# Decayed keys on ScalarE, a reordered first block, a new order of loads and state products behind the attention of step 1

## Chip, cores, metric

The kernel runs on one core of one Trainium2 chip. The metric is the device time of one execution in microseconds (us), the median of several executions. The profiled execution has a span (first to last instruction) that is some 2 us shorter than the time of the same execution. All runs that are compared here are fast runs (a run is called slow when it is over 1.5% above the fastest of its kernel), except where a single run is named as such.

## The reference, cut to what matters

Linear attention with a decay per head, over 6 steps of 128 positions in the kernel (the reference uses blocks of 64, the mathematics is the same), then a gated feed-forward layer.

```python
# q, k, v: (4 batches, 8 heads, 768, 64) f32; lam: one decay per head
for b in range(nb):
    intra = (qb @ kb^T * Dmask) @ vb              # Dmask = lam ** (i - j), lower triangle
    inter = (qb * lam_pow) @ kv_state
    out[:, :, sl] = intra + inter
    kb_dec = kb * rev_pow                         # the decayed keys, "kd" below
    kv_state = lam_block * kv_state + kb_dec^T @ vb
# x = the heads side by side: (3072, 512); weights 512x1536 and 1536x512
out = (sigmoid(x @ w_gate) * (x @ w_val)) @ w_out
```

## The kernel before

Everything is scheduled by hand: each engine executes its instructions in the order in which the program emits them. Names to know:

- `k`, `q`, `v` of a step n are loaded by GpSimd's DMA queue with a cast to bf16; a full load of one of them moves 4 x 8 x 128 = 4096 rows of 64 elements. I write k2, q2, v2 for the loads of step 2.
- From step 2 on, q and k are transposed by DMA (`xbar`, tiles `qt` and `kt`), issued on SyncE's queue.
- `QS` is the scaled q (VectorE), `sp` the scores (TensorE), `MT` the masked scores (VectorE), `op` the attention output (TensorE), `XT` its copy as input of the feed-forward layer.
- `gp`, `vp` are the gate and value products of one unit of 128 feed-forward columns (12 units per step), `sg` the sigmoid (ScalarE), `ht` their product (VectorE), `po` the output projection.
- `cp` is the state product kd^T v of one batch (TensorE). `sd` is the old state times its decay (GpSimd), and VectorE adds both into the state `Sb`.

```python
ps_ff = ctx.enter_context(tc.tile_pool(name="ps_ff", bufs=3, ...))   # gp, vp, po: three PSUM buffers

def make_kd(n):                                   # decayed keys, GpSimd
    KD[n] = kdp.tile([128, B, H, D], BF16, ...)
    nc.gpsimd.tensor_tensor(out=KD[n], in0=T_["k", n], in1=kds..., op=ALU.mult)

def xbar(n):                                      # q first, then k
    for c, d in (("q", QT), ("k", KT)):
        ...
        nc.sync.dma_start_transpose(out=d[n]..., in_=T_[c, n]...)

def piece_c(n, bs):                               # state products and state update
    for b in bs:
        ...                                       # cp = kd^T v, TensorE
        if n > 0:
            nc.gpsimd.tensor_tensor(out=sd, in0=Sb[:, b], in1=dec..., op=ALU.mult)
        for u in range(2):
            ...
            nc.vector.tensor_tensor(out=Sb[us, b, :, us], in0=cp[...], in1=sd[...], op=ALU.add)

# first block, cut: for each batch b of 0, 1 all in turn
for b in range(2):
    cast_hw("k", b); t_("k", 0, [b]); e_k(0, [b]); t_("q", 0, [b]); e_q(0, [b])
    if b == 0:
        make_mask()
    zeros(2)                                      # dummy matmuls that keep TensorE busy
# ... scores, masks, second half ...
# loads, in GpSimd's order, cut
make_kd(0)
# ... weights, k/q/v of step 1 ...
load_wo(0, 6); load_wo(6, 12)
load(2, "qk")
make_kd(1)
load(2, "v")
# step 1, cut: products of the state behind units 0 and 1; in the middle the projections of step 0
for ft in range(4):
    gv(1, ft, *more[ft][:1] if ft < 2 else [lambda: xbar(2)] if ft == 3 else [])
for tt in range(B):
    po(0, tt, *loads if tt == 1 else [])          # loads: load(3, "qkv"), make_kd(2)
# ... units 4 to 11 of step 1; the scores of step 2 stand behind unit 6 ...
```

Of the kernel before, what the change touches and what calls it, by code (L numbers as in the profile page):

```python
# [11 lines left out]
ALU = mybir.AluOpType  # L12
# [4 lines left out]
def kernel(  # L17
# [11 lines left out]
    nc = tc.nc  # L29

    B, H, S, D = q.shape
    C = 128
    NSTEP = S // C
# [9 lines left out]
    qkv = ctx.enter_context(tc.tile_pool(name="qkv", bufs=5))  # L43
# [16 lines left out]
    FIRST_XBAR = 2  # L60
# [8 lines left out]
    T_ = {}  # L69

    def load(n, what, b0=0, b1=B):
        sl = slice(n * C, (n + 1) * C)
        for c in what:
            if (c, n) not in T_:
                T_[c, n] = qkv.tile([128, B, H, D], BF16, tag=c + "b", name=c + "b",
                                      bufs=5 if c == "v" else 4)
            src = {"q": q, "k": k, "v": v}[c]
            nc.gpsimd.dma_start(  # L78
                out=T_[c, n][:, b0:b1],
                in_=src[b0:b1, :, sl, :].rearrange("b h s d -> s (b h) d"))  # L80

    def load_gv(f0, f1):
        fs = slice(f0 * 128, f1 * 128)
        nc.gpsimd.dma_start(out=WG[:, :, fs], in_=wg_r[:, :, fs])  # L84
        nc.gpsimd.dma_start(out=WV[:, :, fs], in_=wv_r[:, :, fs])
# [5 lines left out]
    KD = {}  # L91

    def make_kd(n):
        KD[n] = kdp.tile([128, B, H, D], BF16, tag="kd", name="kd")
        nc.gpsimd.tensor_tensor(  # L95
            out=KD[n], in0=T_["k", n],
            in1=kds.unsqueeze(1).unsqueeze(3).to_broadcast([128, B, H, D]), op=ALU.mult)



# [51 lines left out]
    kds = const.tile([128, H], FP32, tag="kds")  # L152
# [8 lines left out]
    def make_mask():  # L161
        nc.vector.tensor_tensor(  # L162
            out=mask, in0=tri.unsqueeze(1).unsqueeze(1).to_broadcast([128, 2, HP, C]),
            in1=pk.rearrange("p (hp u) -> p u hp", u=2).unsqueeze(3).to_broadcast([128, 2, HP, C]),
            op=ALU.mult)
# [3 lines left out]
    QS, KS, MT, XT, SP, OP = {}, {}, {}, {}, {}, {}  # L169
# [3 lines left out]
    def t_(c, n, bs):  # L173
        ps = ps_at.tile([128, len(bs), HP, C], BF16, name="t" + c, tag="ps")
        for i, b in enumerate(bs):
            for hp in range(HP):
                nc.tensor.transpose(ps[:, i, hp, :], T_[c, n][:, b, 2 * hp:2 * hp + 2, :], ident)  # L177
        (tqs if c == "q" else tks)[n, bs[0]] = ps
# [10 lines left out]
    def e_k(n, bs, parts=1):  # L189
        t = trsb.tile([128, 2, HP, C], BF16, tag="KS", name="KS")  # L190
        w = len(bs) // parts
        for i in range(parts):
            nc.scalar.copy(t[:, i * w:(i + 1) * w], tks[n, bs[0]][:, i * w:(i + 1) * w])  # L193
        for i in range(len(bs)):
            KS[n, bs[i]] = t[:, i]
# [4 lines left out]
    def xbar(n):  # L200
        for c, d in (("q", QT), ("k", KT)):
            d[n] = qtp.tile([128, B, HP, C], BF16, tag=c + "t", name=c + "t")
            nc.sync.dma_start_transpose(
                out=d[n].rearrange("p b hp s -> p (b hp) s"),
                in_=T_[c, n].rearrange("p b h d -> p (b h d)"))
        for b in range(B):
            KS[n, b] = KT[n][:, b]
# [17 lines left out]
    def piece_a(n, bs):  # L225
        for b in bs:
            OP[n, b] = ps_at.tile([128, HP, C], FP32, name="op", tag="ps")
            for hp in range(HP if n > 0 else 0):
                nc.tensor.matmul(OP[n, b][:, hp, :], lhsT=Sb[:, b, hp, :], rhs=QS[n, b][:, hp, :],  # L229
                                 start=(hp == 0), stop=False, skip_group_check=True)  # L230
        for b in bs:
            for hp in range(HP):
                for u in range(2):
                    us = slice(u * 64, (u + 1) * 64)
                    nc.tensor.matmul(OP[n, b][us, hp, :], lhsT=T_["v", n][:, b, 2 * hp + u, :],  # L235
                                     rhs=MT[n, b][:, u, hp, :],
                                     start=(n == 0 and hp == 0), stop=(hp == HP - 1),
                                     skip_group_check=True)

    def piece_x(n, bs):  # L240
        if n not in XT:
            XT[n] = xtp.tile([128, NMT, B, C], BF16, tag="XT", name="XT")
        for b in bs:
            if n < FIRST_XBAR and b % 2:
                nc.vector.tensor_copy(XT[n][:, :, b, :], OP[n, b])  # L245
            else:
                nc.scalar.copy(XT[n][:, :, b, :], OP[n, b])  # L247

    def piece_c(n, bs):
        for b in bs:  # L250
# [56 lines left out]
    def zeros(m):  # L307
        for _ in range(m):
            nc.tensor.matmul(zps, lhsT=Sb[:, 0, 0, :], rhs=Sb[:, 0], start=True, stop=True)  # L309

    zeros(6)
    for b in range(2):
        cast_hw("k", b)
        t_("k", 0, [b])
        e_k(0, [b])
        t_("q", 0, [b])
        e_q(0, [b])
        if b == 0:
            make_mask()
        zeros(2)  # L320
    for b in range(2):
        piece_s(0, [b])
        piece_m(0, b)
        zeros(1)
    t_("k", 0, [2, 3])
    e_k(0, [2, 3], parts=2)
    zeros(1)
    t_("q", 0, [2, 3])
    e_q(0, [2, 3])
    tables_late()  # L330
    zeros(2)
    for b in range(2, 4):
        piece_s(0, [b])
        piece_m(0, b)
    for b in range(B):
        piece_a(0, [b])
        piece_x(0, [b])
        if b:
            zeros(1)
    zeros(2)  # L340



    make_kd(0)
    load_gv(6, 8)
    load(1, "k", 0, 2)
    load(1, "q", 0, 2)
    load_gv(8, 9)
    load(1, "k", 2, 4)
    load(1, "q", 2, 4)  # L350
    load_gv(9, 10)
    load_gv(10, 12)
    load(1, "v")
    load_wo(0, 6)
    load_wo(6, 12)
    load(2, "qk")
    make_kd(1)
    load(2, "v")



# [5 lines left out]
    def gv(n, ft, *more):  # L367
        unit(lambda: piece_gv(n, ft), *more)

    def po(n, tt, *more, cuts=(0, 512)):  # L370
        unit(lambda: piece_po(n, tt, cuts), *more)

    def pair(f, n, bp):
        return lambda: f(n, [2 * bp, 2 * bp + 1])

    def m_(n, b):
        return lambda: piece_m(n, b)

    def trans(n, bp):
        def go():  # L380
            bs = [2 * bp, 2 * bp + 1]
            t_("k", n, bs)
            e_k(n, bs)
            t_("q", n, bs)
            e_q(n, bs)
        return go

    def att(n):
        def go():
            piece_a(n, range(B))  # L390
            piece_x(n, range(B))
        return go

    behind = {ft: [] for ft in range(NFT)}
    behind[3] = [pair(piece_c, 0, 0)]
    behind[4] = [pair(piece_c, 0, 1)]
    behind[7] = [trans(1, 0)]
    behind[8] = [pair(piece_s, 1, 0), m_(1, 0), m_(1, 1), trans(1, 1)]
    behind[9] = [pair(piece_s, 1, 1), m_(1, 2), m_(1, 3)]
    behind[11] = [att(1)]  # L400
    for ft in range(NFT):
        gv(0, ft, *behind[ft])

    for n in range(1, NSTEP):
        nx = n + 1
        more = {i: [] for i in range(NFT)}
        if nx < NSTEP:
            more[0] = [pair(piece_c, n, 0)]
            more[1] = [pair(piece_c, n, 1)]
            more[3] = [lambda nx=nx: e_q(nx, [0, 1])]  # L410
            more[4] = [pair(piece_s, nx, 0), m_(nx, 0)]
            more[5] = [m_(nx, 1), lambda nx=nx: e_q(nx, [2, 3])]
            more[7] = [pair(piece_s, nx, 1), m_(nx, 2)]
            more[8] = [m_(nx, 3)]
            more[11] = [att(nx)]
        loads = [lambda nx=nx: load(nx + 1, "qkv"), lambda nx=nx: make_kd(nx)] if nx + 1 < NSTEP \
            else [lambda nx=nx: make_kd(nx)] if nx < NSTEP - 1 else []
        if n == 1:
            for ft in range(4):
                gv(1, ft, *more[ft][:1] if ft < 2 else [lambda: xbar(2)] if ft == 3 else [])  # L420
            for tt in range(B):
                po(0, tt, *loads if tt == 1 else [])
            gv(1, 4, *more[3])
            gv(1, 5)
            gv(1, 6, *more[4])
            gv(1, 7, *more[5])
            gv(1, 8)
            gv(1, 9, *more[7])
            gv(1, 10, *more[8], lambda: xbar(3))
            gv(1, 11, *more[11])  # L430
        else:
            if nx < NSTEP:
                more[2] += loads
            if nx + 1 < NSTEP:
                more[8].append(lambda nx=nx: xbar(nx + 1))
            for ft in range(NFT):
                gv(n, ft, *more[ft])
        for tt in range(B):
            last = n == NSTEP - 1 and tt == B - 1
            po(n, tt, cuts=(0, 256, 512) if last else (0, 512))  # L440
# [35 lines left out]
```

## Time and profile before

| | before |
|---|---|
| time, median (3 runs) | 240.88 us (240.4 to 241.86) |
| span of the profiled run | 237.8 us |
| TensorE busy | 222.0 us, 93% |
| first gate product starts | 21.32 us |

How to read it: if TensorE is busy 93% of the span, only a change that fills or removes one of its holes matters, and the holes have to be looked at one by one. The page's head, the row of the DMA engines in 40 slices of the span (9 means at least 90% busy), and its chain of waits (PE is TensorE, PEld its weight loads, DVE VectorE, ACT ScalarE, POOL GpSimd, SPq SyncE's DMA queue):

```profile
span 237.8 us, 3703 instructions
...
PE 222.0 (93%) x1479; PEld 111.5 (47%) x1504; DVE 111.6 (47%) x184; ACT 76.5 (32%) x134; POOL 82.0 (34%) x70
...
DMA  7999999999999999999902560002200002200022
...
PE 86%; DVE 8%; DMA 3%; issue 2%; DVEq 0%; POOLq 0%
```

DMA is full in the first 20 slices of 5.9 us. In the timeline of TensorE (start, duration, engine, source line, operation, output and inputs, count, and in brackets the idle time in front and what ended it) the first gate product, the two largest holes behind it, and two other places are these:

```profile
21.32 1.02 PE L278 MATMUL gp<-XT,WG 128*128 128x512 bf16 x4 [0.15 <-DVE XT L245]
...
49.67 1.04 PE L278 MATMUL gp<-XT,WG 128*128 128x512 bf16 x3 [0.94 <-DVE XT L245]
...
55.76 1.03 PE L278 MATMUL gp<-XT,WG 128*128 128x512 bf16 x4
...
73.12 0.62 PE L215 MATMUL sp<-QS,kt 64*128 64x128 bf16 x16
...
112.72 0.62 PE L215 MATMUL sp<-QS,kt 64*128 64x128 bf16 x16 [1.84 <-DVE QS L184]
```

The hole of 1.84 us at 112.7 us waits for a QS of VectorE. The timelines of GpSimd and of VectorE around it, one fence each:

```profile
108.46 3.65 POOL L95 TENSOR_TENSOR kd<-kb,kds 128x2048 bf16<-128x2048 bf16 x1
```

```profile
109.33 3.33 DVE L184 TENSOR_TENSOR QS<-qt,lamq 128x1024 bf16<-128x1024 bf16 x1
```

From step 2 on the same operation takes 0.68 to 0.69 us elsewhere, but for one of 1.85 us at 70.4 us that ran beside an sd; here it ends 0.5 us after kd ends. The last thing to read is GpSimd's timeline in the middle of step 1:

```profile
43.44 1.74 POOL L78 DMA_DIRECT2D vb<-in_v_dram  x1 [0.68 <-DVE ht L287]
45.20 4.03 POOL L258 TENSOR_TENSOR sd<-Sb,dec 128x512 f32<-128x512 bf16 x4
54.76 1.74 POOL L78 DMA_DIRECT2D qb<-in_q_dram  x1 [5.53 <-issue]
58.26 1.68 POOL L78 DMA_DIRECT2D kb<-in_k_dram  x1 [1.75 <-issue]
63.43 1.68 POOL L78 DMA_DIRECT2D vb<-in_v_dram  x1 [3.50 <-PE po L295]
65.13 3.63 POOL L95 TENSOR_TENSOR kd<-kb,kds 128x2048 bf16<-128x2048 bf16 x1
```

Here "issue" means that the profile shows nothing for which the engine waited. The list of DMA issues, asked for the time around the issues of q2 and k2 (35.75 and 37.43 us), gives the time from issue to landing in its last column:

```profile
qb<-in_q_dram POOLq DMA_DIRECT2D x1, 512.0 KB, 18.7
kb<-in_k_dram POOLq DMA_DIRECT2D x1, 512.0 KB, 20.5
```

So q2 landed at 54.45 us, and q3 was issued at 54.76; k2 landed at 57.9, and k3 was issued at 58.26. The releaser that the profile infers for v3 (a projection) is a coincidence: v2 landed at 63.1.

### The profile page before, as it was taken

What the parts mean: (1) busy time and instruction counts of PE and PEld (TensorE: products, weight loads), DVE (VectorE), ACT (ScalarE), POOL (GpSimd) and SP (SyncE); (2) the same over time, 40 slices, a digit from 0 to 9 for tenths busy, and PEclk for the clock granted to TensorE, in tenths of its full rate; (3) what the DMA queues carried; (4) which work ended last, traced back from release to release, by engine and by line L of the source; (5) the groups of instructions that cost most, each with busy time, mean ns of one, the idle gap of its engine ahead of it and who ended that gap; (6) DMA issues with size and microseconds to landing.
All of it is one profiled execution on the core that took longest, in us unless ns stands there. A gap on an engine that the chain in (4) does not pass through costs nothing.

```text
span 237.8 us, 3703 instructions
## 1 busy us (share of the span) xinstructions
PE 222.0 (93%) x1479; PEld 111.5 (47%) x1504; DVE 111.6 (47%) x184; ACT 76.5 (32%) x134; POOL 82.0 (34%) x70
## 2 busy tenths in 40 slices
PE   4498999989999999996999999999999999999994
PEld 1254455544444454543464544464544464444443
DVE  3366476857028810589720388710488710234300
ACT  5233334332133341332342233342233352333211
POOL 8959989824495253398000050000000000000000
PEclk9769999999999999999999999999999999999999
DMA  7999999999999999999902560002200002200022
GB/s 112 152 168 178 161 167 177 206 169 157 143 152 256 136 158 182 230 168 151 106 0 91 145 119 1 3 0 91 88 0 0 3 0 90 91 0 0 0 91 88
DMA packets 104529, 25.15 MB, mean 106 GB/s; under 512 B 95680, under 2 KB 101568, under 8 KB 104512
## 3 DMA queue, kind: packets, MB, share of 16 engines
q0 software_dynamic: 82048, 13.90, 81.1%
q1 hardware_dynamic: 22320, 11.01, 21.2%
q8 instruction: 12, 0.20, 0.4%
q14 instruction: 5, 0.04, 0.0%
q10 hardware_dynamic: 144, 0.00, 0.0%
HBM read 28.32 MB, written 6.29 MB: 146 GB/s over the span
## 4 chain that ended last, share of the span: by engine, by line
PE 86%; DVE 8%; DMA 3%; issue 2%; DVEq 0%; POOLq 0%
PE po L295 26%; PE gp L278 25%; PE vp L284 25%; DVE MT L223 4%; DMA qb<-in_q_dram 3%; PE sp L215 3%; DVE QS L184 2%; PE op L235 2%; PE op L229 2%; PE cp L253 2%; DVE XT L245 1%; PE tq L177 1%; DVE mask L162 1%; PE tk L177 0%; PE zps L309 0%
## 5 line engine op out<-in xcount | busy, mean ns | idle before, releaser
L287 DVE TENSOR_TENSOR ht<-sg,vp 128x512 bf16<-128x512 bf16 x72 | 49.3, 686 | 102.3 <-PE vp L284 101.9
L278 PE MATMUL gp<-XT,WG 128*128 128x512 bf16 x277 | 72.8, 379 | 1.7 <-DVE XT L245 1.1
L284 PE MATMUL vp<-XT,WV 128*128 128x512 bf16 x282 | 73.4, 379 | 0.4
L281 ACT ACTIVATE sg<-gp 128x512 bf16<-128x512 f32 x72 | 43.0, 597 | 90.1 <-PE gp L278 89.3
L295 PE MATMUL po<-WO,ht 128*128 128x512 bf16 (+1 forms) x294 | 62.7, 370 | 0.4 <-issue 0.2
L295 PEld LDWEIGHTS <-ht 128*128 128x128 bf16 x300 | 28.9, 97 | 32.6
L284 PEld LDWEIGHTS <-WV 128*128 128x128 bf16 x288 | 28.2, 98 | 34.0
L278 PEld LDWEIGHTS <-WG 128*128 128x128 bf16 x288 | 26.8, 98 | 31.2 <-DVE XT L245 1.1
L223 DVE TENSOR_TENSOR MT<-sp,mask 128x512 bf16<-128x512 f32 x48 | 30.4, 682 | 1.4 <-PE sp L215 1.4
L300 ACT COPY ob<-po 128x512 f32<-128x512 f32 (+1 forms) x24 | 13.9, 577 | 45.7 <-PE po L295 45.7
L258 POOL TENSOR_TENSOR sd<-Sb,dec 128x512 f32<-128x512 bf16 x16 | 16.7, 1068 | 32.6 <-DVE Sb L266 32.6
L95 POOL TENSOR_TENSOR kd<-kb,kds 128x2048 bf16<-128x2048 bf16 x5 | 18.2, 3636 | 0.8 <-ACT dec L158 0.7
L78 POOL DMA_DIRECT2D qb<-in_q_dram x8 | 11.8, 1474 | 7.2 <-issue 5.5
L266 DVE TENSOR_TENSOR Sb<-cp,sd 64x256 bf16<-64x256 f32 x32 | 13.5, 421 | 0.8
L78 POOL DMA_DIRECT2D vb<-in_v_dram x7 | 10.8, 1541 | 8.0 <-issue 3.8
L247 ACT CAST XT<-op 128x512 bf16<-128x512 f32 x20 | 10.5, 597 | 8.0 <-PE op L235 8.0
L78 POOL DMA_DIRECT2D kb<-in_k_dram x7 | 10.3, 1469 | 7.5 <-issue 7.5
L309 PE MATMUL zps<-Sb 128*128 128x512 bf16 x18 | 7.6, 526 | 2.1 <-DVE Sb L122 2.1
L184 DVE TENSOR_TENSOR QS<-qt,lamq 128x1024 bf16<-128x1024 bf16 x8 | 9.3, 1159 | 0.0
L235 PE MATMUL op<-MT,vb 128*64 128x128 bf16 x192 | 7.3, 221 | 0.7 <-DVE MT L223 0.7
L193 ACT COPY KS<-tk 128x512 bf16<-128x512 bf16 (+1 forms) x6 | 4.3, 729 | 10.4 <-PE tk L177 10.4
L84 POOL DMA_DIRECT2D WG<-in_moe_w_gate_dram x8 | 6.4, 794 | 1.1 <-DMA vb<-in_v_dram 1.1
(41 smaller groups left out, 82.0 us busy)
## 6 DMA issues: line engine op xcount, KB each, us to landing
out_dram<-ob SPq DMA_DIRECT2D x23, 256.0 KB, 2.2
vb<-in_v_dram POOLq DMA_DIRECT2D x5, 512.0 KB, 16.0
qb<-in_q_dram POOLq DMA_DIRECT2D x4, 512.0 KB, 17.8
kb<-in_k_dram POOLq DMA_DIRECT2D x4, 512.0 KB, 18.4
WO<-in_moe_w_out_dram POOLq DMA_DIRECT2D x2, 768.0 KB, 15.0
qb<-in_q_dram POOLq DMA_DIRECT2D x4, 256.0 KB, 7.1
WG<-in_moe_w_gate_dram POOLq DMA_DIRECT2D x4, 256.0 KB, 7.8
WV<-in_moe_w_val_dram POOLq DMA_DIRECT2D x4, 256.0 KB, 8.4
```

The costliest lines, as they stand in the source:

```text
L78: nc.gpsimd.dma_start(out=T_[c, n][:, b0:b1], in_=src[b0:b1, :, sl, :].rearrange("b h s d -> s (b h) d"))
L95: nc.gpsimd.tensor_tensor(out=KD[n], in0=T_["k", n], in1=kds.unsqueeze(1).unsqueeze(3).to_broadcast([128, B, H, D]), op=ALU.mult)
L184: nc.vector.tensor_tensor(out=t[:, :w], in0=src, in1=lamq.unsqueeze(1).to_broadcast([128, w, HP, C]), op=ALU.mult)
L223: nc.vector.tensor_tensor(out=MT[n, b][:, u], in0=SP[n, b][u], in1=mask[:, u], op=ALU.mult)
L258: nc.gpsimd.tensor_tensor(out=sd, in0=Sb[:, b], in1=dec.unsqueeze(2).to_broadcast([128, HP, 128]), op=ALU.mult)
L266: nc.vector.tensor_tensor(out=Sb[us, b, :, us], in0=cp[us, :, us], in1=sd[us, :, us], op=ALU.add)
L278: nc.tensor.matmul(gp, lhsT=WG[:, mt, fs], rhs=x[:, mt, :], start=(mt == 0), stop=(mt == NMT - 1))
L281: nc.scalar.activation(sg, gp, AF.Sigmoid)
L284: nc.tensor.matmul(vp, lhsT=WV[:, mt, fs], rhs=x[:, mt, :], start=(mt == 0), stop=(mt == NMT - 1))
L287: nc.vector.tensor_mul(HT[n, ft], sg, vp)
L295: nc.tensor.matmul(po[:, :c1 - c0], lhsT=HT[n, ft][:, tt * 128:(tt + 1) * 128], rhs=WO[:, ft, c0:c1], start=(ft == 0), stop=(ft == NFT - 1))
L300: nc.scalar.copy(ob[:, c0:c1], po[:, :c1 - c0])
```

## The change

Intent: start the feed-forward layer earlier by ordering each engine's first work by the landing of its data; take the decayed keys from GpSimd, where they hold up VectorE, and make them on ScalarE in pairs of heads; issue loads earlier and k first; and put the state products of step 1 into the wait for XT.

```diff
     def make_kd(n):
         KD[n] = kdp.tile([128, B, H, D], BF16, tag="kd", name="kd")
-        nc.gpsimd.tensor_tensor(
-            out=KD[n], in0=T_["k", n],
-            in1=kds.unsqueeze(1).unsqueeze(3).to_broadcast([128, B, H, D]), op=ALU.mult)
+
+    def piece_kd(n, hs):
+        for h in hs:
+            nc.scalar.mul(KD[n][:, :, h, :], T_["k", n][:, :, h, :], kds[:, h:h + 1])
 ...
+        zeros(2)
+    make_mask()
+    for b in range(2):
         t_("q", 0, [b])
         e_q(0, [b])
-        if b == 0:
-            make_mask()
-        zeros(2)
 ...                       (more of the first block; XT of batch 1 goes to ScalarE)
-    load(2, "qk")
-    make_kd(1)
-    load(2, "v")
+    load(2, "kqv")
+    load(3, "kq")
 ...                       (pairs of kd behind units of step 0 and of later steps)
-    behind[11] = [att(1)]
+    behind[11] = [kd(1, 6), att(1), pair(piece_c, 1, 0), pair(piece_c, 1, 1)]
 ...
+        def loads(nx=nx):
+            if nx < NSTEP - 1:
+                make_kd(nx)
+                load(nx + 1, "v")
+            if nx + 2 < NSTEP:
+                load(nx + 2, "kq")
+
         if n == 1:
             for ft in range(4):
-                gv(1, ft, *more[ft][:1] if ft < 2 else [lambda: xbar(2)] if ft == 3 else [])
+                gv(1, ft)
             for tt in range(B):
-                po(0, tt, *loads if tt == 1 else [])
+                po(0, tt, *[loads, lambda: xbar(2)] if tt == 0 else [])
 ...
```

In the program this makes GpSimd's order v1, w_out, k2, q2, v2, k3, q3, then the four `sd` of step 1; VectorE's order has the eight state updates of step 1 directly behind XT, in front of the first `ht` of step 1; SyncE's order has the first store of an output in front of the transposes of step 2.

More of the change, by code (lines that the diff above doesn't have):

```diff
@@ L238, in piece_a, with piece_x @@
                                      skip_group_check=True)
-    def piece_x(n, bs):
+    def piece_x(n, bs, eng=None):
         if n not in XT:
@@ L243, in piece_x @@
         for b in bs:
-            if n < FIRST_XBAR and b % 2:
-                nc.vector.tensor_copy(XT[n][:, :, b, :], OP[n, b])
-            else:
-                nc.scalar.copy(XT[n][:, :, b, :], OP[n, b])
+            e = eng or (nc.vector if n < FIRST_XBAR and b % 2 else nc.scalar)
+            (e.tensor_copy if e is nc.vector else e.copy)(XT[n][:, :, b, :], OP[n, b])
     def piece_c(n, bs):
@@ L315 @@
         e_k(0, [b])
+        zeros(2)
+    make_mask()
+    for b in range(2):
         t_("q", 0, [b])
         e_q(0, [b])
-        if b == 0:
-            make_mask()
-        zeros(2)
+    zeros(1)
     for b in range(2):
@@ L323 @@
         piece_m(0, b)
-        zeros(1)
     t_("k", 0, [2, 3])
     e_k(0, [2, 3], parts=2)
-    zeros(1)
+    zeros(3)
     t_("q", 0, [2, 3])
@@ L330 @@
     tables_late()
-    zeros(2)
+    zeros(3)
     for b in range(2, 4):
@@ L334 @@
         piece_m(0, b)
-    for b in range(B):
+    for b in range(2):
         piece_a(0, [b])
-        piece_x(0, [b])
-        if b:
-            zeros(1)
+        piece_x(0, [b], nc.scalar)
+    zeros(3)
+    piece_a(0, [2])
+    piece_x(0, [2], nc.scalar)
+    zeros(1)
+    piece_a(0, [3])
+    piece_x(0, [3], nc.vector)
     zeros(2)
-    make_kd(0)
+    for n in range(2):
+        make_kd(n)
     load_gv(6, 8)
@@ L347 @@
     load(1, "q", 0, 2)
-    load_gv(8, 9)
+    load_gv(8, 10)
     load(1, "k", 2, 4)
     load(1, "q", 2, 4)
-    load_gv(9, 10)
     load_gv(10, 12)
@@ L392, in att, with kd @@
         return go
+    def kd(n, h0):
+        return lambda: piece_kd(n, [h0, h0 + 1])
     behind = {ft: [] for ft in range(NFT)}
-    behind[3] = [pair(piece_c, 0, 0)]
-    behind[4] = [pair(piece_c, 0, 1)]
+    for ft in range(4):
+        behind[ft] = [kd(0, 2 * ft)]
+    behind[4] = [pair(piece_c, 0, 0)]
+    behind[5] = [pair(piece_c, 0, 1)]
     behind[7] = [trans(1, 0)]
-    behind[8] = [pair(piece_s, 1, 0), m_(1, 0), m_(1, 1), trans(1, 1)]
-    behind[9] = [pair(piece_s, 1, 1), m_(1, 2), m_(1, 3)]
-    behind[11] = [att(1)]
+    behind[8] = [pair(piece_s, 1, 0), m_(1, 0), m_(1, 1)]
+    behind[9] = [trans(1, 1), kd(1, 0)]
+    behind[10] = [pair(piece_s, 1, 1), m_(1, 2), m_(1, 3), kd(1, 2), kd(1, 4)]
+    behind[11] = [kd(1, 6), att(1), pair(piece_c, 1, 0), pair(piece_c, 1, 1)]
     for ft in range(NFT):
@@ L407 @@
         if nx < NSTEP:
-            more[0] = [pair(piece_c, n, 0)]
-            more[1] = [pair(piece_c, n, 1)]
+            if n > 1:
+                more[0] = [pair(piece_c, n, 0)]
+                more[1] = [pair(piece_c, n, 1)]
             more[3] = [lambda nx=nx: e_q(nx, [0, 1])]
@@ L415 @@
             more[11] = [att(nx)]
-        loads = [lambda nx=nx: load(nx + 1, "qkv"), lambda nx=nx: make_kd(nx)] if nx + 1 < NSTEP \
-            else [lambda nx=nx: make_kd(nx)] if nx < NSTEP - 1 else []
+        if nx < NSTEP - 1:
+            for i in range(4):
+                more[6 + i].append(kd(nx, 2 * i))
+        if nx + 1 < NSTEP:
+            more[9].append(lambda nx=nx: xbar(nx + 1))
+        def loads(nx=nx):
+            if nx < NSTEP - 1:
+                make_kd(nx)
+                load(nx + 1, "v")
+            if nx + 2 < NSTEP:
+                load(nx + 2, "kq")
         if n == 1:
             for ft in range(4):
-                gv(1, ft, *more[ft][:1] if ft < 2 else [lambda: xbar(2)] if ft == 3 else [])
+                gv(1, ft)
             for tt in range(B):
-                po(0, tt, *loads if tt == 1 else [])
+                po(0, tt, *[loads, lambda: xbar(2)] if tt == 0 else [])
             gv(1, 4, *more[3])
@@ L426 @@
             gv(1, 7, *more[5])
-            gv(1, 8)
+            gv(1, 8, *more[6])
             gv(1, 9, *more[7])
-            gv(1, 10, *more[8], lambda: xbar(3))
-            gv(1, 11, *more[11])
-        else:
-            if nx < NSTEP:
-                more[2] += loads
-            if nx + 1 < NSTEP:
-                more[8].append(lambda nx=nx: xbar(nx + 1))
+            gv(1, 10, *more[8])
+            gv(1, 11, *more[9], *more[10], *more[11])
+        else:
+            more[2].append(loads)
             for ft in range(NFT):
```

## The prediction

> **What bounds it.** TensorE. The engine table has PE busy 222.0 of 237.8 us, and the chain of waits is 86% PE. The rest is one prologue (the first gate product starts at 21.3 us) and few later holes, read in PE's timeline: 1.84 us at 112.7 (waiting for the decayed queries QS), 0.94 us at 49.7 (waiting for XT), about 0.7 us more. DMA is full up to about 113 us.
>
> **What the change removes.**
> - Prologue: mask and casts now precede QS; VectorE keeps one XT of two. Its chain (eight MT of 0.62 us, QS 0.69, two XT 0.64) starts when q lands at 8.1 us instead of 12.5: estimate 2 to 3 us earlier.
> - kd leaves GpSimd (3.63 us each). In VectorE's timeline one QS took 3.33 instead of 0.69 us exactly while kd ran at 108.5; that made the 1.84 us hole. The Trainium skill, "SBUF — State Buffer", summary rules, says such pairs block each other; the trace agrees. On ScalarE a pair of heads should cost about 0.85 us (estimate from the 0.32 us of a 128-wide scaled ACTIVATE and the 0.60 us of a 512-wide one); it fits beside a 0.60 us sigmoid in a 1.73 us unit.
> - The 0.94 us XT hole is filled with 0.9 us of state products.
>
> **What it adds: a GpSimd queue that blocks.** The order of instructions on GpSimd becomes k2, q2, v2, k3, q3, and only then the four sd (Sb times decay) of step 1. Before, sd came right after v2 (45.2 to 49.2 us). In before, every fourth full q/k/v load waits for the landing of the oldest of three: q3 issued at 54.76 (q2 landed at 54.45), k3 at 58.26 (57.9), v3 at 63.43 (63.1), v4 at 85.88 (85.5), with no semaphore wait open, and GpSimd stands still meanwhile. The skill ("DMA: Bandwidth & Descriptors", SWDGE part; 16 KiB of descriptor scratch in "SBUF — State Buffer", size table) explains it: 16 partitions x 16 KiB / 16 B gives 16384 descriptors, estimate; a load has 4096 rows, so four do not fit.
>
> So k3 waits for k2 (about 53.7), q3 for q2 (about 57), sd runs 59 to 63. VectorE has the eight Sb updates of step 1 ahead of ht(1,0), so ht(1,0) ends near 64.7. PE has three PSUM buffers: it does two units and stops at about 50.4, for about 14 us. The third gate product of step 1, at 54.0 before, comes at about 64.7: +10.7, whatever the prologue gained. Cold clock after the hole: +2 (estimate from the 6.8 us at half clock in the prologue).
>
> Then the transposes of step 2 stand behind the first output store, so start near 75 instead of 54.4. Before they landed 17.8 us after that start under load; PE wants them 13 us later: a second hole of about 5 us. The later 1.84 us hole goes.
>
> **Prediction.** 240.9 + 10.7 + 2 + 5 - 2, rounded: 257 us, 8 in 10 between 248 and 263. Faster by over 2%: 0.06; within 2%: 0.07; slower: 0.87.
>
> **Right if:** GpSimd issues k3 and q3 near 54 and 57; sd starts near 59; VectorE waits about 10 us for sd in the table of waits; PE has one hole above 8 us near 50 to 64, and one near 86 to 92 before the scores of step 2; first gate product at 18 to 20; no QS above 2 us.
>
> **Wrong if:** the waits before the fourth load are not a full ring, or loads land much sooner, so sd is early; then the gains alone stand, about 236. The second hole is the least sure part: with less traffic it vanishes, leaving about 251.

## The result, and the profile after

| | before | after |
|---|---|---|
| time, median (4 runs each) | 240.64 us (240.06 to 241.86) | 256.56 us (256.34 to 256.76) |
| ratio of fast runs | | 1.0654 (95%: 1.061 to 1.0698) |
| span of the profiled run | 237.8 us | 255.0 us |
| mean granted clock of TensorE (share of full speed) | 0.985 | 0.96 |

A ratio is the mean time of one kernel's fast runs over that of the other's fast runs of the same rounds, so it is not quite the ratio of the medians.

The same views of the changed kernel. The page:

```profile
span 255.0 us, 3744 instructions
...
PE 225.4 (88%) x1482; PEld 112.6 (44%) x1507; DVE 107.8 (42%) x183; ACT 92.7 (36%) x175; POOL 61.7 (24%) x63
...
PE 65%; DMA 12%; POOL 9%; issue 8%; SPq 3%; DVE 1%; ACT 0%; POOLq 0%
```

TensorE's share of the chain fell from 86% to 65%; DMA, GpSimd and unexplained issue time came in. TensorE's timeline:

```profile
17.62 1.02 PE L277 MATMUL gp<-XT,WG 128*128 128x512 bf16 x4 [0.34 <-DVE XT L246]
...
44.34 1.07 PE L252 MATMUL cp<-vb,kd 128*128 128x128 bf16 x16
45.34 1.02 PE L277 MATMUL gp<-XT,WG 128*128 128x512 bf16 x3
...
50.51 1.02 PE L283 MATMUL vp<-XT,WV 128*128 128x512 bf16 x4 [0.69 <-ACT sg L280]
64.42 1.87 PE L277 MATMUL gp<-XT,WG 128*128 128x512 bf16 x4 [12.89 <-DVE ht L286]
...
89.89 1.04 PE L216 MATMUL sp<-QS,kt 64*128 64x128 bf16 x16 [6.60 <-DMA kt<-kb]
```

The first block's gain is there (17.62 instead of 21.32 us), the hole for XT is filled with cp, and two new holes stand behind it: 12.89 us, ended by an `ht`, and 6.60 us, ended by the landing of the transposed k. What VectorE waited for, in its timeline:

```profile
44.00 1.29 DVE L246 CAST XT<-op 128x512 bf16<-128x512 f32 x2
59.80 3.85 DVE L265 TENSOR_TENSOR Sb<-cp,sd 64x256 bf16<-64x256 f32 x8 [14.51 <-POOL sd L257]
63.68 1.88 DVE L286 TENSOR_TENSOR ht<-sg,vp 128x512 bf16<-128x512 bf16 x3
```

And what GpSimd did in the meantime:

```profile
41.86 1.68 POOL L78 DMA_DIRECT2D vb<-in_v_dram  x1 [4.34 <-issue]
53.43 1.67 POOL L78 DMA_DIRECT2D kb<-in_k_dram  x1 [9.89 <-issue]
57.01 1.68 POOL L78 DMA_DIRECT2D qb<-in_q_dram  x1 [1.91 <-issue]
58.71 4.03 POOL L257 TENSOR_TENSOR sd<-Sb,dec 128x512 f32<-128x512 bf16 x4
```

It stood still for 9.89 us with nothing visible to wait for, then issued k3, then q3, and only then made sd. The list of DMA issues for 32 to 36 us gives the landings of k2 (issued at 32.62) and q2 (at 35.85):

```profile
kb<-in_k_dram POOLq DMA_DIRECT2D x1, 512.0 KB, 20.5
qb<-in_q_dram POOLq DMA_DIRECT2D x1, 512.0 KB, 20.9
```

So k2 landed at 53.12 us and k3 was issued 0.31 us later; q2 landed at 56.75 and q3 was issued 0.26 us later. The transposes of step 2, in the timeline of SyncE's DMA queue, came behind the first store:

```profile
70.99 0.36 SPq L300 DMA_DIRECT2D out_dram<-ob  x1
71.40 6.23 SPq L204 DMA_TRANSPOSE qt<-qb  x1
77.67 6.57 SPq L204 DMA_TRANSPOSE kt<-kb  x1
```

and the issues of 71 to 79 us show 13.3 us to landing for the first and 12.2 us for the second: 77.67 + 12.2 = 89.87 us, the moment at which TensorE's second hole ends.

Where the time went, by reading the start of the same instructions in the two timelines of TensorE:

| TensorE starts | before | after | after minus before | step |
|---|---|---|---|---|
| first gate product | 21.32 | 17.62 | -3.70 | -3.70 first block |
| attention of step 1 (op with the state) | 46.66 | 42.33 | -4.33 | -0.63 small waits |
| fourth gate product of step 1 | 55.76 | 64.42 | +8.66 | +12.99 first hole (12.89) and a wait of 0.69, less the XT hole (0.94); 0.35 is not placed |
| first projection of step 0 | 57.48 | 67.59 | +10.11 | +1.45 slow clock |
| first scores of step 2 | 73.12 | 89.89 | +16.77 | +6.66 second hole |
| second scores of step 2 | 78.96 | 98.02 | +19.06 | +2.29 slow clock |
| end | 237.8 | 255.0 | +17.2 | -1.86 no hole for QS at 112.7 |

### The profile page after: what moved, and what is told of

The parts are those of the page before. It is cut to its first block, busy times and chain, and to the rows that moved or that the text cites. A ratio compares the mean times of both kernels' runs of the same rounds, so it can differ in the third digit from the quotient of the medians.

```text
span 255.0 us, 3744 instructions
## 1 busy us (share of the span) xinstructions
PE 225.4 (88%) x1482; PEld 112.6 (44%) x1507; DVE 107.8 (42%) x183; ACT 92.7 (36%) x175; POOL 61.7 (24%) x63
## 4 chain that ended last, share of the span: by engine, by line
PE 65%; DMA 12%; POOL 9%; issue 8%; SPq 3%; DVE 1%; ACT 0%; POOLq 0%
PE po L294 21%; PE gp L277 19%; PE vp L283 19%; DMA kt<-kb 5%; DMA WV<-in_moe_w_val_dram 4%; DMA vb<-in_v_dram 3%; POOL qb L78 2%; SPq L204 2%; POOL kb L78 2%; PE sp L216 2%; PE op L236 2%; PE op L230 1%; POOL sd L257 1%; POOL vb L78 1%; PE cp L252 1%
## 5 line engine op out<-in xcount | busy, mean ns | idle before, releaser
L277 PE MATMUL gp<-XT,WG 128*128 128x512 bf16 x277 | 74.7, 387 | 13.6 <-DVE ht L286 12.9
L283 PE MATMUL vp<-XT,WV 128*128 128x512 bf16 x282 | 75.0, 385 | 1.2 <-ACT sg L280 0.7
L294 PE MATMUL po<-WO,ht 128*128 128x512 bf16 (+1 forms) x294 | 62.7, 370 | 0.4 <-issue 0.2
L98 ACT ACTIVATE kd<-kb,kds 128x256 bf16<-128x256 bf16 x40 | 17.8, 498 | 0.0
L216 PE MATMUL sp<-QS,kt 64*128 64x128 bf16 x128 | 5.4, 229 | 6.6 <-DMA kt<-kb 6.6
L216 PEld LDWEIGHTS <-kt 64*128 64x128 bf16 x128 | 3.9, 99 | 10.1 <-DMA kt<-kb 7.1
L185 DVE TENSOR_TENSOR QS<-qt,lamq 128x1024 bf16<-128x1024 bf16 x8 | 5.5, 684 | 4.1 <-DMA qt<-qb 4.1
```

The lines of the kernel that those rows point to most:

```text
L98: nc.scalar.mul(KD[n][:, :, h, :], T_["k", n][:, :, h, :], kds[:, h:h + 1])
L216: nc.tensor.matmul(sp[u][:, hp, :], lhsT=KS[n, b][us, hp, :], rhs=QS[n, b][us, hp, :], start=(hp == 0), stop=(hp == HP - 1), skip_group_ch ...
L277: nc.tensor.matmul(gp, lhsT=WG[:, mt, fs], rhs=x[:, mt, :], start=(mt == 0), stop=(mt == NMT - 1))
L283: nc.tensor.matmul(vp, lhsT=WV[:, mt, fs], rhs=x[:, mt, :], start=(mt == 0), stop=(mt == NMT - 1))
L294: nc.tensor.matmul(po[:, :c1 - c0], lhsT=HT[n, ft][:, tt * 128:(tt + 1) * 128], rhs=WO[:, ft, c0:c1], start=(ft == 0), stop=(ft == NFT - 1))
```

## The experiments

Theory: GpSimd executes in order, the loads k3 and q3 wait for room in a full descriptor ring, sd waits behind them, VectorE's state updates wait for sd, `ht` waits behind the updates, and TensorE runs out of PSUM buffers. The second hole follows from it: the transposes start late and share the DMA engines with loads. Rivals: the moved state products alone are the cause; the wait is a limit on the number of loads in flight, or on their bytes, not on rows; the transposes are slow by themselves. Eight kernels were run, all correct; they fall into two groups, each on one chip with its own runs of the kernel before.

### 1. sd_first: the loads of step 3 behind sd again

```diff
     load(2, "kqv")
-    load(3, "kq")
 ...
                 make_kd(nx)
-                load(nx + 1, "v")
-            if nx + 2 < NSTEP:
-                load(nx + 2, "kq")
+                load(nx + 1, "kqv")
```

> The changed kernel with one thing undone: the loads of step 3 (k, q, v) stand behind the four sd of step 1 on GpSimd, as they did before; later steps likewise. Theory (full descriptor ring in front of sd): sd of step 1 runs at about 43.6 to 47.6 us, right after v2 is issued; VectorE waits under 1 us for sd instead of 14.5; the 12.9 us hole of PE before the third gate product of step 1 goes, and that product starts near 48.8 us instead of 64.4. Step 2's transposes then start near 56 us and still share the DMA with loads, so a hole of 4 to 6 us before the scores of step 2 stays. Time 237 to 241 us. Rival (the eight Sb updates on VectorE ahead of ht(1,0), from moving the state products together, make the hole whatever sd does): the hole shrinks by at most 4 us and the time stays above 250 us.

Measured: 242.2 us median, ratio to before 1.0062 (1.0014 to 1.0109). The first hole is gone: sd ran at 44.15 us, VectorE's updates followed at 45.29 without a wait, and the third gate product of step 1 started at 48.88 us (expected near 48.8). GpSimd's timeline of this kernel shows that the same wait now stands behind sd, where nobody needs GpSimd:

```profile
42.46 1.67 POOL L78 DMA_DIRECT2D vb<-in_v_dram  x1 [4.36 <-DVE MT L224]
44.15 4.03 POOL L257 TENSOR_TENSOR sd<-Sb,dec 128x512 f32<-128x512 bf16 x4
53.85 1.75 POOL L78 DMA_DIRECT2D kb<-in_k_dram  x1 [5.67 <-issue]
```

The rival that blames the moved products falls: they are still moved here, and no hole follows them. The time missed its range (237 to 241 us) by 1.2 us; the second hole is larger than expected, in TensorE's timeline:

```profile
75.40 1.03 PE L216 MATMUL sp<-QS,kt 64*128 64x128 bf16 x16 [7.25 <-DMA kt<-kb]
```

7.25 us instead of 4 to 6, with a granted clock of 0.70 between 65 and 80 us. The transposes of step 2, in the issues of 57 to 64 us, took this long to land:

```profile
qt<-qb SPq DMA_TRANSPOSE x1, 12.7
kt<-kb SPq DMA_TRANSPOSE x1, 12.2
```

So undoing the first hole alone gives back nearly all of the loss, but leaves none of the gain.

### 2. held: the loads of step 3 held until the transposes of step 2 have landed

On top of sd_first. The held copy is a tiny GpSimd operation that reads the transposed k, and so waits for it.

```diff
+    held = const.tile([128, 2], BF16, tag="held")
 ...
                 make_kd(nx)
+                if nx == 2:
+                    nc.gpsimd.tensor_copy(held, KT[2][:, B - 1, HP - 1, C - 2:C])
                 load(nx + 1, "kqv")
 ...
-                po(0, tt, *[loads, lambda: xbar(2)] if tt == 0 else [])
+                po(0, tt, *[lambda: xbar(2), loads] if tt == 0 else [])
```

> As sd_first, and the loads of step 3 are held on GpSimd, by a copy of two columns of the transposed k of step 2, until that step's transposes have landed; the transposes stand ahead of the loads. Theory (the second hole is the transposes sharing the DMA with the loads): transposed q lands within 8 us and transposed k within 12 us of the transposes' start near 56 us instead of 13.3 and 18.5, the hole before the scores of step 2 is under 1 us, and the time is 232.5 to 235 us, faster than the kernel before. Rival (the transposes are slow by themselves, or start too late): transposed k still lands 16 us or more after the start, a hole of 4 us or more stays, and the time is that of sd_first or more, as the loads of step 3 come later.

Measured: 232.65 us median (231.75 to 233.02), ratio to before 0.9659 (0.9608 to 0.971): faster than both kernels. TensorE's timeline lists no hole after its first gate product (17.87 us), and TensorE is 97% busy. The issues of 56 to 61 us, with their time to landing:

```profile
out_dram<-ob SPq DMA_DIRECT2D x1, 256.0 KB, 3.4
qt<-qb SPq DMA_TRANSPOSE x1, 5.0
kt<-kb SPq DMA_TRANSPOSE x1, 4.4
```

The transposes were issued at 56.30 and 59.45 us, 0.8 us earlier than in sd_first for the first one (57.13), but took 5.0 and 4.4 us where sd_first shows 12.7 and 12.2. The transposes are not slow by themselves; the loads beside them make them slow. The edit also moves the transposes' place in the program; as their start moved by under 1 us, that part can't explain a landing of kt at 63.85 instead of 75.34 us.

### 3. halves: the two loads ahead of sd cut into halves

```diff
-    load(3, "kq")
+    for c in "kq":
+        load(3, c, 0, 2)
+        load(3, c, 2, 4)
```

> The changed kernel with the loads k3 and q3, ahead of sd, each cut into two of half as many rows (2048). Theory (a ring of about 16384 descriptors, a row of a load taking one): with k2, q2, v2 outstanding (12288) a half fits, so the first half of k3 is issued right behind v2, near 43.6 us, with no wait; its second half waits for the landing of k2, near 53 us; the first half of q3 follows at once and its second half waits for q2, near 56.7 us. sd still starts near 58 us, the hole of PE stays above 11 us and the time is 254 to 258 us. Rival (a limit of three loads outstanding, whatever their rows): the first half of k3 also waits until near 53 us.

Measured: 257.66 us, one run. GpSimd's timeline:

```profile
41.87 1.67 POOL L78 DMA_DIRECT2D vb<-in_v_dram  x1 [4.34 <-issue]
43.53 1.15 POOL L78 DMA_DIRECT2D kb<-in_k_dram  x1
53.69 1.14 POOL L78 DMA_DIRECT2D kb<-in_k_dram  x1 [9.00 <-issue]
54.82 1.16 POOL L78 DMA_DIRECT2D qb<-in_q_dram  x1
57.27 1.14 POOL L78 DMA_DIRECT2D qb<-in_q_dram  x1 [1.29 <-issue]
```

Half a load goes out at once behind three whole ones (14336 rows outstanding); the next half, which would make it 16384, waits 9.00 us, until k2 has landed (53.33 us in the list of issues). That is not a limit on the number of loads: once k2 has landed, the first half of q3 goes out as the fifth in flight. At least 14336 rows fit and 16384 do not. Since a half has half the bytes too, halves alone doesn't tell rows from bytes, but the trace of after does: there q2 was issued at 35.85 us while v1 (landed at 41.56), both loads of w_out (768 KB each, landed at about 47) and k2 were on their way, 3072 KB at least with q2 itself, where four loads of 512 KB are refused. Nor did VectorE hold GpSimd up: in after it was idle itself for 14.51 us around that wait. The hole before the fourth gate product stays (12.11 us), as sd still comes at 58.42 us.

### 4. prods_back: the state products of step 1 back behind units 0 and 1

```diff
-    behind[11] = [kd(1, 6), att(1), pair(piece_c, 1, 0), pair(piece_c, 1, 1)]
+    behind[11] = [kd(1, 6), att(1)]
 ...
-            if n > 1:
+            if n > 0:
 ...
-                gv(1, ft)
+                gv(1, ft, *more[ft] if ft < 2 else [])
```

> The changed kernel with the state products of step 1 put back behind the first two units of step 1, load order kept. Theory (sd late because of the loads ahead of it): sd still runs at about 58.7 to 62.7 us, VectorE still waits for it over 9 us; PE gets one unit further before it stops, so the time falls by 2 to 5 us, to 251 to 255 us. Rival (the moved products are the cause): no hole above 3 us before the projections of step 0 and a time of 245 us or less.

Measured: 252.94 us, one run. sd still ran at 58.88 to 62.9 us, and VectorE still waited 11.4 us for it. TensorE got one unit further before it stopped, and its hole, now in front of the projections, is 7.95 us; the second one is 6.92 us:

```profile
62.61 12.16 PE L294 MATMUL po<-WO,ht 128*128 128x512 bf16 x48 [7.95 <-DVE ht L286]
```

So the place of the products sets how far TensorE gets, and the loads ahead of sd set when it goes on.

### 5. prologue: the new first block alone, on the kernel before

The edit takes the changed kernel's first block and `piece_x` into the kernel before, and nothing else. Its core:

```diff
         cast_hw("k", b)
         t_("k", 0, [b])
         e_k(0, [b])
+        zeros(2)
+    make_mask()
+    for b in range(2):
         t_("q", 0, [b])
         e_q(0, [b])
-        if b == 0:
-            make_mask()
-        zeros(2)
 ...
-    for b in range(B):
+    for b in range(2):
         piece_a(0, [b])
-        piece_x(0, [b])
+        piece_x(0, [b], nc.scalar)
 ...
```

> The kernel before with the new order of the first block alone. Theory (transposes of step 2, bound by landings of q2 and k2 and by the loads beside them, are the next limit): the first gate product starts at 17.6 to 18.2 us instead of 21.3, a gain of 3.2 to 3.7 us; transposed k still lands near 72 us, so a new hole of 2 to 4 us opens before the scores of step 2; the time is 238.5 to 240.7 us, within 1% of before. Rival (the gain of the prologue carries to the end): 236.5 to 237.5 us and no new hole.

Measured: 240.41 us median, ratio 0.9993 (0.9965 to 1.0021): the same time, although the first gate product starts at 18.12 us, 3.2 us earlier. TensorE's timeline has the new hole where it was expected, and the old one for QS:

```profile
72.11 0.62 PE L215 MATMUL sp<-QS,kt 64*128 64x128 bf16 x16 [2.11 <-DMA kt<-kb]
...
113.40 0.62 PE L215 MATMUL sp<-QS,kt 64*128 64x128 bf16 x16 [1.85 <-DVE QS L184]
```

Transposed k landed at 72.0 us, as in before (72.2). So 3.2 us of gain met a landing that did not move: 1.0 us is left when those scores start (72.11 instead of 73.12), and the granted clock takes more than the rest: the gate product behind the hole takes 1.88 us, where one took 1.04, and the second scores of step 2 start at 79.64 instead of 78.96.

### 6 to 8. held with one part of the change undone each

held_old_prologue puts the old first block back:

```diff
         cast_hw("k", b)
         t_("k", 0, [b])
         e_k(0, [b])
-        zeros(2)
-    make_mask()
-    for b in range(2):
         t_("q", 0, [b])
         e_q(0, [b])
+        if b == 0:
+            make_mask()
+        zeros(2)
 ...
```

> The kernel held with the old order of the first block. Theory: where the loads no longer stand in the way the prologue's gain carries through, so this is 3.2 to 3.9 us slower than held: 235.8 to 236.8 us. Rival (held is limited elsewhere): within 1.5 us of held.

Measured: 235.68 us, ratio to before 0.9796 (0.9767 to 0.9826). Against held's 0.9659, measured in the other group, the first block is worth about 1.4% or 3.3 us (0.9796 - 0.9659, times 240.5). The time is 0.12 us below the expected range. The two traces say the same without comparing groups: the first gate product starts at 21.15 us here and at 17.87 in held, 3.28 us apart, and neither timeline lists a hole behind it.

held_kd_pool makes kd of steps 2 to 4 on GpSimd again, behind that step's loads:

```diff
     def make_kd(n):
         KD[n] = kdp.tile(...)
+        if n < 2:
+            return
+        nc.gpsimd.tensor_tensor(out=KD[n], in0=T_["k", n], in1=kds..., op=ALU.mult)
 ...
-                make_kd(nx)
                 ...
                 load(nx + 1, "kqv")
+                make_kd(nx)
```

> The kernel held with the decayed keys of steps 2 to 4 on GpSimd again, behind that step's loads. Theory (VectorE's QS, which reads two operands of SBUF, stands still while a GpSimd operation on SBUF runs): kd of step 4 runs at about 103.6 to 107.2 us and the QS at 104.5 us takes 2.5 to 3.5 us instead of 0.68; PE gets a hole of 1 to 2.5 us after it; the time is 233.8 to 236.5 us. Rival (kd on GpSimd costs nothing): no QS above 1.6 us, time within 0.5 us of held.

Measured: 235.61 us (234.14 to 238.1, one of six runs slow), ratio of the fast runs 0.9793 (0.9751 to 0.9836), so about 3.2 us dearer than held by the same reckoning. GpSimd (kd of step 4) and VectorE (QS of step 3) at 105 us, one fence each:

```profile
104.39 3.65 POOL L97 TENSOR_TENSOR kd<-kb,kds 128x2048 bf16<-128x2048 bf16 x1
```

```profile
105.28 3.32 DVE L190 TENSOR_TENSOR QS<-qt,lamq 128x1024 bf16<-128x1024 bf16 x1
```

The long QS of before is back, and with it a hole of 1.83 us in TensorE; one of 0.63 us came with a QS of 2.11 us at 72.7. The two holes make 2.46 us; the profiled run (237.18 us, clock 0.993) was the slowest of the fast ones, so its total is not the one to compare. In held the longest QS of step 2 and later was 1.52 us (beside an sd) and cost no hole.

held_prods_back undoes the move of the products with the edit of prods_back.

> The kernel held with the state products of step 1 behind the first two units of step 1 again. Theory (with sd on time the moved products fill 0.9 us in which PE waits for XT): a hole of 0.7 to 1.0 us at about 45 us and a time 0.6 to 1.1 us above held. Rival (the move is worth nothing): within 0.3 us.

Measured: 233.8 us, ratio 0.9705 (0.9671 to 0.974). The trace shows the 0.94 us hole for XT again, at 45.8 us. The time differs from held by 1.15 us in the median (expected 0.6 to 1.1), but the two were measured in different groups and their intervals overlap: the hole is shown, its worth in time is likely but not settled.

## Why the prediction was right

The time (256.56 us against 257) and its mechanism were right. That the number came within half a microsecond is luck. By the table, the first block and the first hole together cost 8.66 us (+10.7 in the prediction's sum), the slow clock 3.74 (+2), the second hole 6.66 (+5), and the lost QS hole gave 1.86 (-2). That is 17.2 us between the two profiled runs, where the sum has 15.7. Between the medians it is 15.9, because the profiled run of before (239.67 us) was faster than all four in the result's table and that of after (256.76 us) the slowest of its four.

- **The full ring in front of sd: right.** k3 was predicted near 54 us, q3 near 57, sd from 59 to 63; they came at 53.43, 57.01 and 58.71 to 62.7. halves and the trace of after show that the limit goes by rows: 14336 fit, 16384 do not. This agrees with what the Trainium skill gives: "DMA: Bandwidth & Descriptors", section Terms, a descriptor of 16 bytes, and "SBUF — State Buffer", section "SBUF size: 192, 224, or 256?", a scratch of 16 KiB for descriptors in each partition. The prediction's estimate from them is 16384 descriptors, exactly four loads of 4096 rows, so the estimate alone doesn't decide whether a fourth load fits; the waits in before and in halves do. That what fills up is this ring is inferred from the match; the runs show the limit in rows. sd_first shows that the order of GpSimd's queue, not the amount of work, made the first hole.
- **The size of the first hole: mis-sized.** The prediction said that "PE has three PSUM buffers: it does two units and stops at about 50.4", and put the step at +10.7 us for the third gate product. TensorE did three units and stopped at 51.5; the fourth gate product was delayed by 8.66 us. The trace shows why: the third gate product started at 48.79 us without a wait, while two value products still waited for `ht`, and the third value product started at 50.51 us, after 0.69 us of waiting for a sigmoid. So the buffer that a sigmoid freed was given to the next product, and all three buffers, not two, were in the end held by value products that waited for `ht`.
- **Slow clock: mis-sized.** "+2" for one cold stretch; there were two, +1.45 and +2.29 us. Both holes were followed by matmuls at half clock (granted clock 0.58 from 64 to 68 us, 0.50 and 0.66 from 88 to 96 us). The skill, "TensorE: Matmul & The Clock Gate", section "Part 1: The HAM clock gate", says that an idle array falls to half rate and needs a busy window of 3.4 us. The traces agree on the half rate (0.50). The time at it, counted from the first matmul behind the hole, was 3.0 us behind the first hole and 4.8 us behind the second, so the 3.4 us hold only roughly. A short hole can be enough: the one of 2.11 us in prologue was followed by 3.4 us at half clock, the one of 1.85 us in the same run by none.
- **The second hole: right, a little small.** "About 5 us", called the least sure part; 6.66 us by the table above. Both ends of it came earlier than predicted: the transposes started at 71.40 us (near 75 predicted), and TensorE wanted them at 83.3 us (near 88). Its cause held: with the loads out of the way (held), both transposes land in under half the time.
- **The gains: there, the first larger than predicted, and absorbed.** The first block was worth 3.70 us at the first gate product (predicted 2 to 3), the lost QS hole 1.86 us (predicted 1.84). As predicted, the first gain did not matter, "whatever the prologue gained": the end of the first hole is tied to the landing of q2, and a TensorE that comes earlier only waits longer. prologue shows the same absorption without the ring.
- **kd on ScalarE: right.** A pair of heads took 0.89 to 0.90 us (estimate 0.85); the longest wait that it made was 0.81 us of one `ht` for a sigmoid behind kd, at 40.3 us, without a hole in TensorE; no QS took over 0.70 us. The rule on which the prediction rested, "SBUF — State Buffer", section "Summary: rules for kernel authors", that a VectorE operation with two operands in SBUF blocks while GpSimd reads SBUF, agrees with the traces: 0.68 against 3.3 us, in before and again in held_kd_pool.

What a reader could have taken from the profile of before without running anything: the waits named "issue" in front of loads, each ending 0.3 us after a landing three loads earlier. What the prediction did not get from it was how many products TensorE would still get out.

The version that the experiments point to is held: the change with the loads of step 3 back behind sd and held until the transposes have landed, 232.65 us, 3.4% faster than before.

## What to carry to other kernels

A queue that issues DMAs in order is also a place where compute can get stuck: before moving a load ahead of an operation on the same engine, ask whether there will be room for it when it is reached, and who waits for what stands behind it. A gain at the start of a kernel is worth only what the next fixed landing leaves of it, so find the landing that TensorE meets next before counting the gain. And when bulk loads are far ahead of their use, holding them back until a small transfer on the critical path has landed can be worth more than issuing them early.

## What the Trainium skill lacked or had wrong

- "DMA: Bandwidth & Descriptors" does not say what GpSimd does when its descriptor ring is full. Here it waited in order, with compute behind it standing still (9.89 us), and went on 0.26 to 0.36 us after the landing of the oldest load. "Debugging Trainium Hangs", section "Descriptor Overflow", names too many descriptors for the 16 KiB scratch only as a cause of hangs; here it was a wait, and every result was correct.
- No page gives the number of rows that fit; halves shows that 14336 fit and 16384 do not, over the 16 DMA engines, for rows of 64 elements with a cast.
- "DMA: Bandwidth & Descriptors", section "Rules for kernel authors", says that a transpose next to ordinary DMAs "needs nothing". That holds for the results; in time two transposes of 512 KB took 12.7 and 12.2 us beside a busy load queue (sd_first) and 5.0 and 4.4 us with it empty but for one load, which landed 2.4 us after the first transpose was issued (held).
